# An attention and gated-MLP kernel: hand-set instruction order against a list scheduler with a time model

## The chip, the cores and the metric

The kernel runs on one core of a Trainium2 chip. The metric is the device time of one execution in microseconds (us), taken over several executions. The core has a matmul engine (PE, with weight loads listed as PEld), a vector engine (DVE), an activation engine (ACT), GpSimd (POOL) and a queue engine (SP) that issues the transfers. Each of them has its own instruction stream, whose order the program sets, and waits on semaphores for the others. The matmuls of this kernel write to PSUM, of which it uses eight banks. PE is called cold here where its granted clock was 0.50, half of full speed, and warm at 1.00.

A run is called slow when it is over 1.5% above the fastest of the same kernel in its set. The kernel before read between 619.6 and 631.7 us over all chips used here. Its profiled run, 629.58 us, carries the mark slow for that reason, in the set where 619.6 was the fastest; a fast run of a variant with the same early part shows the same early stretches (it is shown at its place below).

## The reference

```python
x  = A_x                                   # 1 x 2048 x 448, bf16
xn = layernorm(x)                          # no scale, no shift
q, k, v = split(xn @ wqkv)                 # 16 heads of 28
s  = softmax(q k^T / sqrt(28)) v, heads joined, @ wo
g  = silu(gelu(xn @ w1 + b1) @ w2 + b2)    # 448 -> 1792 -> 448
out = x + s * g
```

The 16 heads of 2048 x 2048 scores are 67 million exponentials. They run on ACT, 128 x 1536 at a time, in 342 instructions (the last is 128 x 512).

## The kernel before

Heads are packed four to a group, four groups, each head padded to 32 columns. A step `u` is three score matmuls of 512 columns, one exponential over the three PSUM banks they fill (a ring of six banks, so two steps), and three PV matmuls into the accumulator bank `acc`. Everything else (transposes of the normalised input, the projections K, Q and V, the MLP's first layer F1 and second layer F2, the softmax denominators, the output projection) is side work. It goes through the one bank that is left, `misc`, in generators that the main loop draws from by a fixed budget in ns per step:

```python
PV_LAG = 2
PV_START = 6
BUDGET0 = 900
BUDGET = 460
...
    def misc_item(self):
        return self.misc[:, :], self.b_misc
...
    def it_k(self, g, c):                   # K of head group g, chunk c of 512 rows
        bank, tok = K.misc_item()
        for k in range(2):
            K.proj_mm(1, g, c, bank, tok, (2 * k, 2 * k + 1))
            if k == 0:
                yield 440
        K.k_ev(DVE, g, c, bank, tok)
        yield 440
...
        for u in range(NU):                 # the main loop
            ...                             # scores of step u, exponential of step u, PV of step u - 2
            early = bool(fill) and u < 26
            bal = min(bal, 0) + (BUDGET0 if early else BUDGET)
            if gelu_it is not None and u == gelu_it + 2:
                bal += 22000
            while bal > 0:
                r = step_fill(u)
                if r is None:
                    break
                bal -= r
            if gelu_it is None and K.n_f1 == C * FT:
                gelu_it = u
                K.gelu()
```

Layernorm runs by chunks of four 128-row tiles: four statistics, one logarithm and one exponential on ACT for the four, four applications. GpSimd sets constants and pads from the start. At the end, the last head block's denominators go through GpSimd, and one dependence tracker per chunk covers the output buffer.

The softmax here doesn't subtract the row's maximum and nothing guards it: scores larger than these inputs give would overflow.

Of the kernel before, what the change touches and what calls it, by code (L numbers as in the profile page):

```python
# [14 lines left out]
D = 448  # L15
H = 16
DH = 28
F = 1792
G = 4
# [14 lines left out]
PV_LAG = 2  # L34
PV_START = 6
BUDGET0 = 900
BUDGET = 460


class _Buf:  # L40
    __slots__ = ("w", "r")

    def __init__(self):
        self.w = None
        self.r = []


class _Kernel:
    def __init__(self, nc, A_x, A_wqkv, A_wo, B_w1, B_b1, B_w2, B_b2, out):
        self.nc = nc  # L50
        self.A_x, self.A_wqkv, self.A_wo = A_x, A_wqkv, A_wo
        self.B_w1, self.B_b1, self.B_w2, self.B_b2 = B_w1, B_b1, B_w2, B_b2
        self.out = out
        self.es = ExitStack()
        self.prog = {PE: [], ACT: [], DVE: [], POOL: [], SP: []}
        self.evsem = {}
        self.evcnt = {}
        self.waited = {E: {} for E in self.prog}

# [16 lines left out]
    def own(self, E, h):  # L76
        return h is not None and h[0] is self.evsem[E]

    def deps(self, E, reads, writes):
        for b in reads:  # L80
            if not (E == PE and self.own(E, b.w)):
                self.wait(E, b.w)
        for b in writes:
            if not (E == PE and self.own(E, b.w)):
                self.wait(E, b.w)
            for r in b.r:
                if not (E == PE and self.own(E, r)):
                    self.wait(E, r)

    def mark(self, h, reads, writes):  # L90
        for b in writes:
            b.w = h
            b.r = []
        for b in reads:
            b.r.append(h)

    def emit(self, E, fn, reads=(), writes=()):
        self.deps(E, reads, writes)
        sem = self.evsem[E]
        self.evcnt[E] += 1  # L100
        self.prog[E].append(lambda eng, f=fn, s=sem: f(eng).then_inc(s, 1))
        h = (sem, self.evcnt[E])
        self.mark(h, reads, writes)
        return h

    def dma(self, E, fn, dsem, reads=(), writes=()):
# [4 lines left out]
        self.mark(h, reads, writes)  # L111
        return h

# [17 lines left out]
    def alloc(self):  # L131
# [18 lines left out]
        self.qsq = sb("qsq", [128, 512], bf)  # L150
# [4 lines left out]
        self.iota_f = sb("iota_f", [128, 128], f32)  # L155
# [22 lines left out]
        self.osb = self.h[:, :, 1792:3584].rearrange("p c (t d) -> p c t d", d=D)  # L178
        self.wsq = self.P[:, 20:24, :]
# [9 lines left out]
        self.b_xn = [B() for _ in range(3)]  # L189
        self.b_xnT = [[B(), B()] for _ in range(C)]  # L190
        self.b_stg, self.b_wv, self.b_w1, self.b_w2, self.b_wo = B(), B(), B(), B(), B()
# [10 lines left out]
        self.b_osb = [B() for _ in range(C)]  # L202
        self.b_E = [B(), B()]
        self.b_qsq, self.b_rc, self.b_rhl, self.b_colK, self.b_csq = B(), B(), B(), B(), B()
        self.b_wsq = [B() for _ in range(G)]
        self.b_st, self.b_mv, self.b_ln, self.b_rs = ([B() for _ in range(C)] for _ in range(4))
        self.b_fsb, self.b_sig = [B(), B()], [B(), B()]
        self.b_dum = B()
        self.s_x = [self.sem("s_x%d" % q) for q in range(4)]
        self.s_out = [self.sem("s_out%d" % q) for q in range(4)]  # L210
        self.s_w = {n: self.sem("s_" + n) for n in ("wqk", "wv", "w1", "w2", "wo", "b")}

    def schedule(self):
        self.constants()
        self.loads()
        self.startup()
        self.main()
        self.finish()

    def constants(self):  # L220
# [3 lines left out]
        def f(eng):  # L224
            eng.memset(K.epsc[:, :], LN_EPS)
            eng.memset(K.dum[:, :], 1.0)
            eng.memset(K.stg[64:128, 3, :, :, :], 0.0)
# [7 lines left out]
            eng.memset(K.ones[:, :], 1.0)  # L235
            return eng.memset(K.xn[:, :, :, D:512], 0.0)
        e(DVE, f, writes=[K.b_pads])

        def f(eng):
            return eng.memset(K.w1[64:128, 3, :], 0.0)  # L240
        e(DVE, f, writes=[K.b_w1])
# [5 lines left out]
        e(POOL, f, writes=[io])  # L247
# [3 lines left out]
        e(POOL, f, reads=[io], writes=[K.b_id])  # L251
        ec, tc = _Buf(), _Buf()
        e(POOL, lambda eng: eng.tensor_copy(K.ecol[:, 0:1], K.iota_p[:, :]), reads=[io], writes=[ec])
        for thr in (32.0, 64.0, 96.0):
            e(POOL, lambda eng, thr=thr: eng.tensor_scalar(K.tcol[:, :], K.iota_p[:, :], thr, 32.0,
                                                           op0=ALU.is_ge, op1=ALU.mult), reads=[io], writes=[tc])
            e(POOL, lambda eng: eng.tensor_tensor(K.ecol[:, 0:1], K.ecol[:, 0:1], K.tcol[:, :], ALU.subtract),
              reads=[ec, tc], writes=[ec])

        def f(eng):  # L260
# [3 lines left out]
        e(POOL, f, reads=[ec, io], writes=[K.b_cols])  # L264
        e(POOL, lambda eng: eng.tensor_scalar(K.tcol[:, :], K.ecol[:, 3:4], 28.0, None, op0=ALU.add),
          reads=[K.b_cols], writes=[tc])
# [4 lines left out]
        e(POOL, f, reads=[K.b_cols], writes=[hm])  # L271
# [4 lines left out]
        e(POOL, f, reads=[tc, hm, io], writes=[K.b_bsel])  # L276
# [3 lines left out]
        e(POOL, f, reads=[K.b_id], writes=[K.b_bsel])  # L280

        def f(eng):
            eng.memset(K.vaug[:, :, :, DH:DH + 1], 2.0)
            return eng.memset(K.vaug[:, :, :, DH + 1:32], 0.0)
        e(POOL, f, writes=[K.b_vpad])
        e(POOL, lambda eng: eng.memset(K.wo[:, :, :], 0.0), writes=[K.b_wo])
        self.prog[ACT].append(lambda eng: eng.preload_act_table_set("natural_log_exp_and_others"))

    def loads(self):
        K = self  # L290

        def ld(dst, src, sem, w):
            return K.dma(SP, lambda eng: eng.dma_start(dst, src), sem, writes=w)
        xr = K.A_x[0].rearrange("(c p t) d -> c p t d", p=128, t=4)
        wq = K.A_wqkv
        ld(K.x_sb[:, 0, :, :], xr[0], K.s_x[0], [K.b_x[0]])
        sf = K.stg.rearrange("p k w h d -> p k (w h d)")
        ld(sf[:, 0:3, :], wq[0:384, 0:2 * D].rearrange("(kt p) n -> p kt n", p=128), K.s_w["wqk"], [])
        ld(sf[0:64, 3, :], wq[384:448, 0:2 * D], K.s_w["wqk"], [K.b_stg])
        ld(K.x_sb[:, 1, :, :], xr[1], K.s_x[1], [K.b_x[1]])  # L300
        ld(K.wv[:, 0:3, 0:D], wq[0:384, 2 * D:3 * D].rearrange("(kt p) n -> p kt n", p=128), K.s_w["wv"], [])
        ld(K.wv[0:64, 3, 0:D], wq[384:448, 2 * D:3 * D], K.s_w["wv"], [K.b_wv])
        for c in (2, 3):
            ld(K.x_sb[:, c, :, :], xr[c], K.s_x[c], [K.b_x[c]])
        with K.nc.allow_non_contiguous_dma(reason="tiny bias load"):
            pass
# [4 lines left out]
        K.dma(SP, f, K.s_w["b"], writes=[K.b_b1])  # L311
        ld(K.b2b[:, :], K.B_b2.partition_broadcast(128), K.s_w["b"], [K.b_b2])
        K.b_b1.w = K.b_b2.w
        ld(K.w1[:, 0:3, :], K.B_w1[0:384, :].rearrange("(kt p) f -> p kt f", p=128), K.s_w["w1"], [])
        ld(K.w1[0:64, 3, :], K.B_w1[384:448, :], K.s_w["w1"], [K.b_w1])
        ld(K.w2[:, :, :], K.B_w2.rearrange("(ft p) d -> p ft d", p=128), K.s_w["w2"], [K.b_w2])
        K.wait(SP, K.b_wo.w)
        K.b_wo.w = None
        for hh in range(H):
            g, j = hh // 4, hh % 4  # L320
            ld(K.wo[32 * j:32 * j + DH, g, :], K.A_wo[hh * DH:(hh + 1) * DH, :], K.s_w["wo"],
               [K.b_wo] if hh == H - 1 else [])

    def ln_stats(self, c):
        K = self
        for t in range(4):
            i = 4 * c + t
            K.emit(DVE, lambda eng, i=i, t=t: eng.bn_stats(K.st6[:, i, :], K.x_sb[:, c, t, :]),
                   reads=[K.b_x[c]], writes=[K.b_st[c]])

        def f(eng):
            ins = None
            for i in range(4 * c, 4 * c + 4):
                ins = eng.bn_aggr(K.mv[:, i, :], K.st6[:, i, :])
            return ins
        K.emit(DVE, f, reads=[K.b_st[c]], writes=[K.b_mv[c]])

    def ln_rstd(self, c):
        K = self
        sl = slice(4 * c, 4 * c + 4)  # L340
        K.emit(ACT, lambda eng: eng.activation(K.lnv[:, sl], K.mv[:, sl, 1], ACTF.Ln, bias=K.epsc[:, 0:1]),
               reads=[K.b_mv[c], K.b_pads], writes=[K.b_ln[c]])
        K.emit(ACT, lambda eng: eng.activation(K.rstd[:, sl], K.lnv[:, sl], ACTF.Exp, scale=-0.5),
               reads=[K.b_ln[c]], writes=[K.b_rs[c]])

    def ln_apply(self, c):
        K = self
        for t in range(4):
            i = 4 * c + t
            K.emit(DVE, lambda eng, i=i, t=t: eng.tensor_scalar(  # L350
                K.xn[:, c % 3, t, 0:D], K.x_sb[:, c, t, :], K.mv[:, i, 0:1], K.rstd[:, i:i + 1],
                op0=ALU.subtract, op1=ALU.mult),
                reads=[K.b_x[c], K.b_mv[c], K.b_rs[c], K.b_pads], writes=[K.b_xn[c % 3]])

    def tr_mm(self, c, pr, bank, tok):
# [3 lines left out]
        def f(eng):  # L359
            ins = None  # L360
            for k in range(2):
                kt = 2 * pr + k
                for t in range(4):
# [3 lines left out]
        K.emit(PE, f, reads=[K.b_xn[c % 3], K.b_id], writes=[tok])  # L367

    def tr_ev(self, E, c, pr, bank, tok):
# [3 lines left out]
        if E == ACT:  # L373
            fn = lambda eng: eng.activation(dst, psb, ACTF.Copy)
        else:
            fn = lambda eng: eng.tensor_copy(dst, psb)
        K.emit(E, fn, reads=[tok], writes=[K.b_xnT[c][pr]])

    def proj_mm(self, which, g, c, bank, tok, kts=range(KT)):
        K = self  # L380
        kts = list(kts)
        w = (K.wq, K.wk)[which]

        def f(eng):
            ins = None
            for kt in kts:
# [14 lines left out]
    def v_mm(self, c, part, bank, tok):  # L401
# [12 lines left out]
        if part == 0:  # L414
            for q in range(2):
# [5 lines left out]
                if q == 0:  # L421
                    yield 500
# [553 lines left out]
```

## Time and profile before

| what | before |
|---|---|
| time, median of its runs | 629.93 us |
| span of the profiled run | 627.6 us |
| first exponential starts | 21.87 us |
| from there to gelu's table load (204 exponentials) | 347.0 us |
| gelu with its two table loads | 27.0 us |
| from there to the end of the last exponential (138) | 212.6 us |
| from there to the end | 19.1 us |
| ACT's waits for score matmuls before exponentials | 86.8 us |

The five stretches add up to the span. When ACT is full, exponentials stand 1.344 us apart, so 204 of them need 274.2 us and 138 need 185.5. What a stretch takes beyond that, 72.8 and 27.1 us here (with 6.8 us of tanh in the second), is what an order could save. The page, the cuts by stretch and the timelines that carry this are shown in the prediction.

### The profile page before, as it was taken

The page shows a single profiled execution, that of the slowest core. Times are in us where ns is not written, and L with a number is a line of the kernel's source. Part 1 is how long each engine was busy: PE and PEld are TensorE (multiplying, and loading weights), DVE is VectorE, ACT ScalarE, POOL GpSimd, SP SyncE. Part 2 cuts the span into 40 slices and gives each one's busy share as a digit, 9 for nine tenths or more (in the row PEclk, how much of TensorE's full clock was granted, in tenths as well). Part 3 has the DMA queues.
Part 4 walks back from the last instruction along what each step waited for, and adds up shares of the span by engine and source line. Part 5 has one row for each costly group of instructions (what it writes and reads, how often), then busy time and mean ns, then how long its engine had stood idle before and what let it go on. Part 6 is the DMA issues. An engine that isn't in the chain of part 4 may idle for free.

```text
span 627.6 us, 7506 instructions
## 1 busy us (share of the span) xinstructions
PE 494.6 (79%) x3074; PEld 142.9 (23%) x3106; DVE 177.8 (28%) x306; ACT 505.9 (81%) x367; POOL 55.6 (9%) x76
## 2 busy tenths in 40 slices
PE   1666778888887888898889848769899689898982
PEld 1232112322222222222222213312222112121220
DVE  7653223223323333323232311131111201121203
ACT  2443334987988999999999999468999999999970
POOL 8000100111110101010010100000010101010101
PEclk9775566997989999999999988978989655757766
DMA  8500000000000000000000000000000000000000
GB/s 257 174 2 1 0 0 1 2 0 1 1 0 2 2 1 1 1 1 0 2 1 1 0 1 0 2 0 2 1 0 1 1 0 2 30 0 30 1 29 29
DMA packets 7201, 9.07 MB, mean 14 GB/s; under 512 B 2304, under 2 KB 5824, under 8 KB 7168
## 3 DMA queue, kind: packets, MB, share of 16 engines
q1 hardware_dynamic: 7168, 8.61, 4.4%
q8 instruction: 24, 0.39, 0.2%
q14 instruction: 9, 0.07, 0.0%
HBM read 6.77 MB, written 1.84 MB: 14 GB/s over the span
## 4 chain that ended last, share of the span: by engine, by line
PE 48%; ACT 20%; DVE 19%; issue 12%; POOL 1%; DMA 0%; POOLq 0%; ACTq 0%; DVEq 0%
ACT P L836 18%; PE acc L784 9%; PE ring L821 9%; PE misc L594 8%; PE misc L629 6%; PE misc L387 6%; DVE h L604 5%; PE misc L410 2%; DVE h L350 2%; DVE qT L578 2%; DVE kT L398 2%; DVE qT L566 2%; PE misc L686 1%; PE misc L706 1%; DVE w L636 1%
## 5 line engine op out<-in xcount | busy, mean ns | idle before, releaser
L836 ACT ACTIVATE P<-ring 128x1536 bf16<-128x1536 f32 x342 | 466.6, 1511 | 87.4 <-PE ring L821 86.8
L821 PE MATMUL ring<-qT,kT 32*128 32x512 bf16 x1024 | 152.7, 440 | 24.7 <-ACT P L836 19.7
L784 PE MATMUL acc<-P,vaug 128*32 128x512 bf16 x1024 | 154.8, 446 | 1.3 <-DVE E_sb L658 1.3
L594 PE MATMUL misc<-xnT,w 128*128 128x512 bf16 x207 | 65.1, 393 | 18.9 <-DVE h L604 8.2
L629 PE MATMUL misc<-w,h 128*128 128x448 bf16 x224 | 56.6, 379 | 20.7 <-DVE w L636 12.0
L821 PEld LDWEIGHTS ring<-qT,kT 32*128 32x128 bf16 x1024 | 34.0, 93 | 163.0 <-ACT P L836 96.7
L604 DVE TENSOR_SCALAR h<-misc,b1c 128x512 bf16<-128x512 f32 x56 | 42.0, 750 | 102.1 <-PE misc L594 102.1
L784 PEld LDWEIGHTS acc<-P,vaug 128*32 128x32 bf16 x1024 | 34.3, 95 | 96.2 <-issue 91.5
L672 POOL CAST rhi<-rc 128x512 bf16<-128x512 f32 x16 | 9.8, 610 | 375.6 <-DVE rc L670 294.6
L636 DVE TENSOR_TENSOR w<-misc,b2b 128x448 bf16<-128x448 f32 x16 | 10.0, 624 | 82.2 <-PE misc L629 82.2
L567 POOL TENSOR_TENSOR qsq<-qT 128x512 bf16<-128x512 bf16 x15 | 15.6, 1039 | 182.0 <-DVE qT L566 182.0
L658 DVE CAST E_sb<-acc 128x512 bf16<-128x512 f32 x16 | 11.0, 690 | 68.7 <-PE acc L784 68.6
L629 PEld LDWEIGHTS misc<-w,h 128*128 128x128 bf16 x224 | 18.0, 100 | 48.3 <-issue 24.0
L410 PE MATMUL misc<-wv,xnT 128*128 128x128 bf16 (+1 forms) x128 | 21.2, 309 | 7.4 <-DVE kT L398 3.3
L387 PE MATMUL misc<-xnT,wk 128*128 128x512 bf16 x52 | 19.9, 465 | 8.0 <-DVE kT L398 2.1
L387 PE MATMUL misc<-xnT,wq 128*128 128x512 bf16 x57 | 21.2, 455 | 5.9 <-DVE kT L398 2.0
L613 ACT ACTIVATE h<-h 128x7168 bf16<-128x7168 bf16 x4 | 24.4, 6164 | 0.0
L594 PEld LDWEIGHTS misc<-xnT,w 128*128 128x128 bf16 x224 | 13.1, 98 | 45.8 <-DVE h L604 17.4
L566 DVE CAST qT<-misc 128x512 bf16<-128x512 f32 x15 | 10.4, 691 | 34.1 <-PE misc L387 34.1
L398 DVE TENSOR_SCALAR kT<-misc,ecol 128x512 bf16<-128x512 f32 x15 | 11.2, 749 | 28.9 <-PE misc L387 25.7
L691 DVE TENSOR_TENSOR qT<-misc,E_sb 128x512 bf16<-128x512 f32 x16 | 11.1, 692 | 29.4 <-PE misc L686 29.4
L439 DVE CAST vaug<-misc 128x336 bf16<-128x336 f32 (+1 forms) x20 | 10.6, 531 | 27.8 <-PE misc L410 27.8
(92 smaller groups left out, 233.0 us busy)
## 6 DMA issues: line engine op xcount, KB each, us to landing
x_sb<-in_A_x_dram SPq DMA_DIRECT2D x4, 448.0 KB, 6.3
w<-in_B_w_dram SPq DMA_DIRECT2D x1, 1568.0 KB, 12.1
w<-in_B_w_dram SPq DMA_DIRECT2D x1, 1344.0 KB, 7.4
out_dram<-h SPq DMA_DIRECT2D x3, 448.0 KB, 2.5
h<-in_A_wqkv_dram SPq DMA_DIRECT2D x1, 672.0 KB, 4.8
out_dram<-h SPq DMA_DIRECT2D x2, 224.0 KB, 1.9
wo<-in_A_wo_dram SPq DMA_DIRECT2D x16, 24.5 KB
wv<-in_A_wqkv_dram SPq DMA_DIRECT2D x1, 336.0 KB, 5.9
```

Source lines behind the costliest of these rows:

```text
L387: ins = eng.matmul(bank, w[:, kt, g * 128:(g + 1) * 128], K.xnT[:, kt, c * 512:(c + 1) * 512], start=(kt == 0), stop=(kt == KT - 1))
L398: fn = lambda eng: eng.tensor_scalar(dst, bank, K.ecol[:, 2:3], None, op0=ALU.add)
L410: ins = eng.matmul(bank[:, off:off + nh * 32], K.xnT[:, kt, t * 128:(t + 1) * 128], ap, start=(kt == 0), stop=(kt == KT - 1), skip_group_c ...
L566: K.emit(DVE, lambda eng: eng.tensor_copy(qb, bank), reads=[tok], writes=[K.b_qT[g][c]])
L594: ins = eng.matmul(bank, K.w1[:, kt, ft * 128:(ft + 1) * 128], K.xnT[:, kt, c * 512:(c + 1) * 512], start=(kt == 0), stop=(kt == KT - 1))
L604: K.emit(DVE, lambda eng: eng.tensor_scalar(dst, bank, K.b1c[:, ft:ft + 1], None, op0=ALU.add), reads=[tok, K.b_b1c], writes=[K.b_h[c]])
L613: K.emit(ACT, lambda eng, hv=hv: eng.activation(hv, hv, ACTF.Gelu_apprx_tanh), reads=[K.b_h[c]], writes=[K.b_h[c]])
L629: ins = eng.matmul(ps, hv[:, ft, t * 128:(t + 1) * 128], K.w2[:, ft, :], start=(ft == 0), stop=(ft == FT - 1))
L636: K.emit(DVE, lambda eng: eng.tensor_tensor(fb, ps, K.b2b[:, :], ALU.add), reads=[tok, K.b_b2], writes=[K.b_fsb[c % 2]])
L784: return eng.matmul(K.acc[32 * j:32 * j + 32, :], K.vaug[:, t, 4 * g + j, :], K.P[:, m % NP, :], tile_position=(0, 32 * j), start=(t == 0) ...
L821: return eng.matmul(K.ring[:, m % NRING, :], K.kT[32 * j:32 * j + 32, g, t * 128:(t + 1) * 128], K.qT[32 * j:32 * j + 32, g, c * 512:(c + ...
L836: return eng.activation(K.P[:, p0:p0 + n, :], K.ring[:, b0:b0 + n, :], ACTF.Exp, scale=SM_SCALE)
```

## The change

The intent: one list scheduler places the instructions of all engines. Every piece of work is a generator that yields tasks with an engine, the buffers read and written, a duration and a priority. The scheduler keeps a time for each engine and buffer and always places the task that can start earliest, lower priority number first among those on the same engine that start within 0.1 us. Scores have priority 1, PV 2, side work 5. With it come: layernorm by pairs of tiles, `acc` lent out as a second side bank until PV takes it, PV started by the scheduler, GpSimd's padding and weight squares held back until the normalised tile is there, the last denominator split on DVE, and output buffers tracked by halves.

```diff
+class _Task:
+    def __init__(self, E, fn, reads=(), writes=(), dur=0.1, lat=0.05, prio=5):
...
+    def start_of(self, t):
+        s = self.tE[t.E]
+        for b in t.reads:
+            if b.tw is None:
+                return None
+            s = max(s, b.tw + SEM)
+        for b in t.writes:
+            s = max(s, (b.tw or 0.0) + (0.0 if t.E == PE else SEM), b.tr + SEM)
+        return s
...
+            s0, p0 = min(cand, key=lambda c: (c[0], c[1][3].prio, c[1][0], c[1][1]))
+            E = p0[3].E
+            near = [c for c in cand if c[1][3].E == E and c[0] <= s0 + EPS]
+            s, p = min(near, key=lambda c: (c[1][3].prio, c[1][0], c[0], c[1][1]))
...
+        self.banks = [(self.misc[:, :], self.b_misc), (self.acc[:, :], self.b_acc)]
...
+    def p_k(self, g, c):
+        bank, tok = yield ("bank", lambda: K.ready(K.b_xnT[c] + [K.b_wqk[1][g]]))
+        for k in range(2):
+            yield K.t_proj(1, g, c, bank, tok, k)
+        yield K.t_kev(DVE, g, c, bank, tok)
+        K.banks.append((bank, tok))
...
+            yield ("until", lambda: K.exp_u >= u - 2)
+            yield _Task(PE, fall, rd, [K.b_ring[m % NRING] for m in ms], 0.31, 0.1, 1)
...
+        yield ("until", lambda: K.exp_u >= PV_START and any(t is K.b_acc for _, t in K.banks))
...
-        self.b_osb = [B() for _ in range(C)]
+        self.b_osb = [[B(), B()] for _ in range(C)]
...
+        En, d1, d2 = (DVE, 0.6, 0.65) if last else (POOL, 0.62, 1.05)
```

## The prediction

> **What bounds the kernel now.** I read the page first: shares, slices, groups.
>
> ```profile
> span 627.6 us, 7506 instructions
> ...
> PE   1666778888887888898889848769899689898982
> ...
> ACT  2443334987988999999999999468999999999970
> ...
> PEclk9775566997989999999999988978989655757766
> ...
> L836 ACT ACTIVATE P<-ring 128x1536 bf16<-128x1536 f32 x342 | 466.6, 1511 | 87.4 <-PE ring L821 86.8
> ```
>
> The softmax exponentials, 342 instructions on ACT, are the floor. ACT is nearly full in most slices and two thirds empty in slices 1 to 6. Its idle time before the exponentials, 86.8 us, is waiting for score matmuls (ring). Next I cut the exponentials by stretches: stretch, its length, ACT's busy time (count), clock.
>
> ```profile
> 22.00:60.00 38.00, 16.56 (x12) 0.69 0.07 19
> 60.00:110.00 50.00, 20.02 (x15) 0.59 0.00 0
> 110.00:160.00 50.00, 42.67 (x32) 0.90 0.00 1
> 160.00:240.00 80.00, 74.07 (x55) 0.98 0.00 1
> 240.00:369.00 129.00, 126.17 (x94) 1.00 0.00 1
> ...
> 396.00:430.00 34.00, 14.54 (x11) 0.80 0.00 1
> 430.00:606.00 176.00, 169.81 (x126) 0.76 0.02 9
> ```
>
> Of the waiting, 51.5 us lie in 22 to 110, about 13 in 110 to 240 (130 less 116.7, tiny operations left aside), and 16.4 in 396 to 430; hardly any from 240 to 369 or after 430. So the steady state is already bound by ACT: only start, gelu and end can give time. The timeline shows why the start is slow:
>
> ```profile
> 62.41 0.61 PE L821 MATMUL ring<-qT,kT 32*128 32x512 bf16 x3
> ...
> 63.49 1.03 PE L387 MATMUL misc<-xnT,wq 128*128 128x512 bf16 x2
> 64.56 0.69 DVE L566 CAST qT<-misc 128x512 bf16<-128x512 f32 x1 [3.18 <-PE misc L387]
> 65.31 1.03 PE L387 MATMUL misc<-xnT,wq 128*128 128x512 bf16 x2 [0.79 <-DVE qT L566]
> 66.28 0.61 PE L821 MATMUL ring<-qT,kT 32*128 32x512 bf16 x3
> ```
>
> Scores are 3.87 us apart though an exponential takes 1.45. Between them PE's in-order queue has two pairs of side matmuls (1.03 each), PV (0.61), and the wait for the one side bank's eviction (0.79). The before kernel sets side work by a fixed budget, 900 per step until step 26 and 460 after; at half clock, 900 is twice what it means.
>
> The span before adds up: first exponential at 21.87; 342 at 1.344 apart (score triples at 599.98, 601.33, 602.67: ACT full) 459.6; gelu with two table loads 27.0 (24.38 + 2 x 1.28); four tanh of 1.70, 6.8; layernorm activations between exponentials 1 (two pairs of 0.5); tail from the last exponential (608.48) 19.1. Sum 535.4. The missing 92.2 is the 86.8 of waits, plus about 0.1 for each of the 57 exponentials that did not follow another directly (1.45 against 1.344).
>
> **What the Trainium skill says.** "TensorE: Matmul & The Clock Gate", Part 1, has the array at half clock by default and full clock after a busy window of some 3.4 us. The trace agrees on two speeds: a score triple takes 0.61 at clock 0.50 and 0.39 at 1.00. It also shows that busy time at half clock need not lift it: 60 to 110 is 76% busy (37.97 of 50) at 0.59. "Perfetto Trace Analysis", Matmuls, advises rotating groups through PSUM banks; the 0.79 above is what one bank costs. "SBUF — State Buffer", Who interferes with whom, says that VectorE in its two-port modes and GpSimd exclude each other for whole instructions. The trace agrees: the four layernorm applications at 7.63 take 6.17 us beside GpSimd's memsets and multiply, the same four 1.68 at 22.76. "ScalarE: Activation LUTs", What ACT_TABLE_LOAD costs, says about 2.7 us; here it is 1.28, which decides.
>
> ```profile
> 7.63 6.17 DVE L350 TENSOR_SCALAR h<-x_sb,mv,rstd 128x448 bf16<-128x448 bf16 x4 [0.68 <-ACT rstd L343]
> ...
> 22.76 1.68 DVE L350 TENSOR_SCALAR h<-x_sb,mv,rstd 128x448 bf16<-128x448 bf16 x4
> ```
>
> **The change, part by part.** The arithmetic is nearly the same; order is what moves. I read the built order of both programs, no times from it.
>
> *Until the first exponential.* GpSimd's padding now waits for the normalised tile, so the four applications should cost 1.7, not 6.17: -4.5. Pairs let the second half's statistics run while ACT does the first half's rstd, but the second half waits on ACT behind a weight copy that needs a load landing at about 7: about -1. Against it, V matmuls (8 of 128 columns, 4 of 384, some 1.5 at half clock) now stand before the first scores: +1. First exponential at 17.4: -4.5. Four layernorm pairs now stand between exponentials: 2 in the sum below, where it was 1.
>
> *Steps 0 to 30.* Counted in the order, gaps between score groups with over 0.75 us of side matmul streaming (columns over 2.4 GHz) number 21 in steps 1 to 27 before and 7 after. Twelve of 64 matmuls for V's other heads stand in steps 20 to 40 where all 64 did; they spread to step 60. But three chunks' transposes, K and V must still come within 16 steps, and the largest gaps (2.13 at step 5, 1.49 at step 10, 1.28 at step 16) each cost one or two exponentials, double if cold. The second bank is used only until step 5: 5 groups of matmuls. PV starts after 5 score steps where it was 7, so "deferred" does not show as a later start. I book these two at 1 us or less. I leave 10 of the 51.5 idle us: -41, and 25 isolated exponentials become packed, -2.
>
> *Steps 30 to gelu.* One pair of side matmuls (about 0.45 warm) per step beside scores and PV (0.33 each), some 1.1 of 1.344, as in 240 to 369, where nothing idles. I leave 4 of 13: -9, with -2 for packing.
>
> *Gelu.* ACT's order has 212 exponentials ahead of it (204 before). Before, a bonus of 22000 put 150 F2 matmuls in front of the next scores, so ACT idled 10.9 us at once, 16.4 in all. Now F2 is spread, 54 to 56 matmuls per 20 steps over steps 220 to 280: 2.8 x 0.19 = 0.53 beside 0.66, which fits. K and Q of the last head group fill PE under gelu. I leave 2: -14, packing -1.
>
> *Tail.* Last PV 0.45; six output matmuls that stand ahead of the denominators, 2.25 at half clock (0.375 each); denominators and reciprocal 0.66; the split of the reciprocal on DVE 1.45 (estimate: as DVE's 0.69 for 512 columns, twice; it was 1.66 on GpSimd with handoffs); broadcast 0.6; multiply 0.75; first output matmul 0.6; four evictions of 1.14; store 2.0. Sum 13.3, against 19.1: -5.8. The 2.08 wait of DVE for the first store, visible below, goes, since the output buffer is now tracked by halves.
>
> ```profile
> 619.79 0.62 DVE L714 TENSOR_TENSOR h<-ring,h 128x448 bf16<-128x448 f32 x1
> 620.45 0.39 DVE L716 TENSOR_TENSOR h<-h,x_sb 128x448 bf16<-128x448 bf16 x1
> 622.93 0.62 DVE L714 TENSOR_TENSOR h<-ring,h 128x448 bf16<-128x448 f32 x1 [2.08 <-DMA out_dram<-h]
> ```
>
> Sum after: 17.4 + 459.6 + 27.0 + 6.8 + 2 + 13.3 = 526.1. Idle left: 10 + 4 + 2, and 2 for the stretch after 430, which I leave as it was: 18. The span is then 544.1. The differences added up (-4.5 - 43 - 11 - 15 - 5.8 = -79.3) give 548.3; they leave the other isolated exponentials as they are, so I take the sum. Runs exceed the span by 1.9 (629.43 to 629.58 against 627.6): **546 us**, a ratio of 0.867.
>
> **Rivals.** *The clock stays half.* The order was made with full-clock durations (0.31 for a triple). If PE stays cold with holes, a step costs 0.6 + 0.6 + 0.85 + handoffs, some 2.1, not 1.344, and 40 to 60 such steps cost 30 to 45: about 580. For: 60 to 110 is cold at 76% busy. Against: with a bank eviction covered by scores and PV, PE has no holes when cold, and the trace shows that full PE warms up (420 to 426 is 100% busy at 0.50, 432 on is 1.00). *The chunk chain in steps 0 to 16 is latency-bound* (layernorm, transpose, evict, project, evict through one bank): before, 22 to 60 had 12 exponentials in 38 us. If only PE's bursts shrink and this chain stays, 10 more us are lost: 555. *Packed solid*: if the order holds, idle falls to 6: 533. *A step order that fits a model but not the chip* makes small waits on every side group: 0.1 on 200 steps is 20: 565.
>
> **Range and chances.** All big terms are waits that the new order removes for plain reasons, with ACT's floor at 526 in span, 528 in time. Low: 532, nearly no idle. High: 562, the chain and some cold stretches. Being within 2% would need 70 of the 92 us to stay; a slower kernel would need new waits. Faster 0.97, same 0.02, slower 0.01.
>
> **What would show it.** First exponential near 17.4 and four applications near 1.7; 22 to 60 holding about 24 exponentials where it held 12; clock above 0.8 from 30 to gelu; no wait near 10.9 after gelu; tail near 13 with no DMA wait on DVE. I am wrong if the clock in 30 to 110 stays near 0.6, if the waits of exponentials for scores stay above 35 us, or if GpSimd now blocks DVE later on the path to the first scores.

## The result and the profile after

The changed kernel took 544.57 us (median of 4 runs, 544.18 to 547.09) against 629.93. The ratio is 0.8658, with a 95% interval of 0.8625 to 0.869. Ratios here are the mean time of one kernel's fast runs over that of the other's in the same rounds, so they are not quite the ratio of the medians quoted. The result was correct, and the profiled run was a fast one. The prediction had 546, and a range of 532 to 562.

The page of the changed kernel, the same lines as of before (busy tenths in 40 slices; PEclk is the clock granted to PE, in tenths of full speed; then the exponentials' group with its busy time, and the idle time ahead of it with what ended it):

```profile
span 542.9 us, 7525 instructions
...
PE   2778899999999999999999966899999998798973
...
ACT  3656999999999999999999999799999999999990
...
PEclk9887999999999999999999985899999999685867
...
L852 ACT ACTIVATE P<-ring 128x1536 bf16<-128x1536 f32 x342 | 462.3, 1851 | 12.5 <-PE ring L830 12.0
```

ACT is full from the fifth slice on (54 us), but for one slice behind gelu. The idle time ahead of the exponentials fell from 87.4 to 12.5 us. PE is busy 87% of the span, and its clock was 1.00 from 60 to 300 us. The exponentials by stretches (stretch, its length, ACT's busy time and count of exponentials, granted clock, two columns of transfers):

```profile
22.00:60.00 38.00, 24.23 (x18) 0.82 0.11 31
60.00:110.00 50.00, 50.00 (x39) 1.00 0.00 1
110.00:160.00 50.00, 50.00 (x39) 1.00 0.00 1
```

From 60 to 110 all 50 us are exponentials where it was 20.02, at clock 1.00 instead of 0.59. From 110 to 300 there is no gap at all. The stretch of 22 to 60 is the one that stays open: 24.23 busy of 38.

| what | before | after | difference |
|---|---|---|---|
| first exponential starts | 21.87 | 17.24 | -4.6 |
| to gelu's table load, beyond 1.344 per exponential | 72.8 | 15.0 | -57.8 |
| gelu and its table loads | 27.0 | 27.0 | 0 |
| from there to the last exponential's end, beyond 1.344 each | 27.1 | 9.9 | -17.2 |
| tail | 19.1 | 14.1 | -5.0 |

The differences sum to 84.6; the spans differ by 84.7. In the two rows of the exponentials, 211 and 131 stand after the change where 204 and 138 stood. ACT's timeline in the open stretch (start, duration, group, and the idle time just before):

```profile
17.24 4.13 ACT L852 ACTIVATE P<-ring 128x1536 bf16<-128x1536 f32 x3 [1.29 <-PE ring L830]
...
22.15 1.43 ACT L852 ACTIVATE P<-ring 128x1536 bf16<-128x1536 f32 x1
...
23.90 1.43 ACT L852 ACTIVATE P<-ring 128x1536 bf16<-128x1536 f32 x1
28.50 0.29 ACT L511 ACTIVATE lnv<-mv,epsc 128x2 f32<-128x2 f32 x1 [3.16 <-DVE mv L503]
...
30.66 0.30 ACT L511 ACTIVATE lnv<-mv,epsc 128x2 f32<-128x2 f32 x1 [1.64 <-DVE mv L503]
...
31.10 6.79 ACT L852 ACTIVATE P<-ring 128x1536 bf16<-128x1536 f32 x5
42.72 8.48 ACT L852 ACTIVATE P<-ring 128x1536 bf16<-128x1536 f32 x6 [4.82 <-PE ring L830]
53.80 67.27 ACT L852 ACTIVATE P<-ring 128x1536 bf16<-128x1536 f32 x50 [2.60 <-PE ring L830]
...
348.40 18.91 ACT L852 ACTIVATE P<-ring 128x1536 bf16<-128x1536 f32 x14 [2.76 <-PE ring L830]
```

The sixth exponential comes at 31.10, though the fifth ended at 25.33; there are waits of 4.82 before the eleventh and 2.60 before the seventeenth. From 53.80 to 315.87 exponentials follow each other without a gap. After gelu one wait of 2.76 us is left, and one of 0.50 at 479.

What PE did while the sixth exponential was waited for (the same columns, all engines):

```profile
24.33 1.86 PE L551 MATMUL misc<-xnT,wk 128*128 128x512 bf16 x4 [0.99 <-DVE xnT L542]
...
24.72 0.68 DVE L542 COPY xnT<-acc 128x1024 bf16<-128x1024 bf16 x1
...
27.95 0.13 PEld L551 LDWEIGHTS misc<-xnT,wk 128*128 128x128 bf16 x2 [0.84 <-DVE st L497]
...
29.73 0.75 DVE L562 TENSOR_SCALAR kT<-misc,ecol 128x512 bf16<-128x512 f32 x1
...
30.53 0.60 PE L830 MATMUL ring<-qT,kT 32*128 32x512 bf16 x6 [0.85 <-DVE kT L562]
```

PE works on a K projection at 24.33, then PV, then on a second K projection at 27.95, whose eviction ends at 30.48, and only then come six score matmuls. In the built order the first of these K projections waits for GpSimd, and GpSimd copies only the weights of the second to fourth head group. So the first one is K of a later group, not wanted before the 86th exponential (a group has four blocks of 64 score matmuls, three to a step). It got the side bank because it was ready when the bank came free; K of the second chunk, which the next scores read, was not ready yet (its second transposed half was evicted from 24.72 to 25.40) and had to wait for the bank, and then for PV's fifteen matmuls (26.13 to 28.03).

The time before the sixth exponential is not in the 12.0 us of waits for scores: ACT's stream has two layernorm pairs there, which wait 3.16 and 1.64 us for DVE. They end with the scores, not long after them. DVE's aggregate for the second pair (30.39) stands behind the eviction of that same K (29.73), and the first exponential started 0.44 us after its score matmuls (16.80 to 17.24); by that distance the sixth, with its scores at 30.53, would have come at 30.97 without layernorm, 0.13 us sooner.

The tail of the changed kernel:

```profile
529.30 0.61 PE L882 MATMUL acc<-P,vaug 128*32 128x512 bf16 x3
...
529.85 1.30 PE L943 MATMUL ring<-wo,qT 128*128 128x448 bf16 x3
...
531.09 0.41 PE L882 MATMUL acc<-P,vaug 128*32 128x512 bf16 x1
...
538.28 0.62 DVE L952 TENSOR_TENSOR h<-ring,h 128x448 bf16<-128x448 f32 x1
```

The last exponential ends at 528.77, but the last PV matmul stands behind two groups of three output matmuls and runs at 531.09. The third of the four output evictions (538.28) follows directly; before, it waited 2.08 us for the first store.

### The profile page after: what moved, and what is told of

It reads as the page before. It is cut to its first block, busy times and chain, and to the rows that moved or that the text cites. A ratio compares the mean times of both kernels' runs of the same rounds, so it can differ in the third digit from the quotient of the medians.

```text
span 542.9 us, 7525 instructions
## 1 busy us (share of the span) xinstructions
PE 469.9 (87%) x3106; PEld 138.4 (25%) x3106; DVE 174.2 (32%) x308; ACT 501.9 (92%) x375; POOL 53.9 (10%) x74
## 4 chain that ended last, share of the span: by engine, by line
ACT 55%; PE 22%; issue 15%; DVE 6%; DMA 1%; SPq 0%; ACTq 0%; DVEq 0%
ACT P L852 54%; PE ring L830 5%; PE acc L882 5%; PE misc L551 4%; PE misc L798 4%; PE misc L943 1%; PE misc L715 1%; DMA h<-in_A_wqkv_dram 1%; DVE kT L562 1%; DVE h L952 1%; DVE h L517 1%; PE ring L551 1%; DVE qT L691 1%; DVE qT L701 1%; PE misc L928 0%
## 5 line engine op out<-in xcount | busy, mean ns | idle before, releaser
L852 ACT ACTIVATE P<-ring 128x1536 bf16<-128x1536 f32 x342 | 462.3, 1851 | 12.5 <-PE ring L830 12.0
L830 PE MATMUL ring<-qT,kT 32*128 32x512 bf16 x1024 | 139.4, 403 | 32.6 <-ACT P L852 21.0
L882 PE MATMUL acc<-P,vaug 128*32 128x512 bf16 x1024 | 142.6, 411 | 0.9 <-ACT P L852 0.7
L755 PE MATMUL misc<-xnT,w 128*128 128x512 bf16 x224 | 66.6, 384 | 1.7
L798 PEld LDWEIGHTS misc<-w,h 128*128 128x128 bf16 x224 | 16.7, 100 | 28.7 <-issue 17.4
L551 PE MATMUL misc<-xnT,wq 128*128 128x512 bf16 x60 | 20.0, 433 | 3.8 <-DVE qT L701 2.5
L755 PEld LDWEIGHTS misc<-xnT,w 128*128 128x128 bf16 x224 | 13.3, 97 | 30.5 <-issue 13.2
L715 PE MATMUL misc<-wv,xnT 128*128 128x384 bf16 (+1 forms) x112 | 17.2, 294 | 0.3
L943 PE MATMUL misc<-wo,qT 128*128 128x448 bf16 x52 | 15.0, 387 | 2.4 <-DVE h L952 1.0
## 6 DMA issues: line engine op xcount, KB each, us to landing
w<-in_B_w_dram SPq DMA_DIRECT2D x1, 1568.0 KB, 14.1
```

What stands on the lines that cost most here:

```text
L551: ins = eng.matmul(bank, w[:, kt, g * 128:(g + 1) * 128], K.xnT[:, kt, c * 512:(c + 1) * 512], start=(kt == 0), stop=(kt == KT - 1))
L715: ins = eng.matmul(bank[:, off:off + nh * 32], K.xnT[:, kt, t * 128:(t + 1) * 128], ap, start=(kt == 0), stop=(kt == KT - 1), skip_group_c ...
L755: ins = eng.matmul(bank, K.w1[:, kt, ft * 128:(ft + 1) * 128], K.xnT[:, kt, c * 512:(c + 1) * 512], start=(kt == 0), stop=(kt == KT - 1))
L798: ins = eng.matmul(ps, hv[:, ft, t * 128:(t + 1) * 128], K.w2[:, ft, :], start=(ft == 0), stop=(ft == FT - 1))
L830: return eng.matmul(K.ring[:, m % NRING, :], K.kT[32 * j:32 * j + 32, g, t * 128:(t + 1) * 128], K.qT[32 * j:32 * j + 32, g, c * 512:(c + ...
L852: return eng.activation(K.P[:, p0:p0 + n, :], K.ring[:, b0:b0 + n, :], ACTF.Exp, scale=SM_SCALE)
```

## The experiments

Twelve runs, all correct. Each is timed against the kernel before in the same rounds. The rounds ran on three chips; across chips the ratios are the safer comparison. A scheduler that places everything anew also moves other work when one part is undone, so an undo is not the old state of that part alone. First come undos of single parts of the change.

**One side bank from the start.**

```diff
-        self.banks = [(self.misc[:, :], self.b_misc), (self.acc[:, :], self.b_acc)]
+        self.banks = [(self.misc[:, :], self.b_misc)]
...
-        yield ("until", lambda: K.exp_u >= PV_START and any(t is K.b_acc for _, t in K.banks))
-        i = [t is K.b_acc for _, t in K.banks].index(True)
-        K.banks.pop(i)
+        yield ("until", lambda: K.exp_u >= PV_START)
```

> The changed kernel with one PSUM bank for side work from the start; the accumulator bank is never lent. My theory, as predicted: the second bank carries only 5 groups of matmuls before step 5, so it is worth 1 us or less: 543 to 547 us, with the exponentials' waits for scores at 11 to 15 us instead of 12.0. Rival: the start was bound by the single bank, and the loan bought much of the early gain: 555 us or more, with waits of 22 us or more before 60.

Measured: 544.51 us (one of the four runs, 550.4, is slow and left out of the ratio), ratio 0.866 (0.8588 to 0.8731), waits of exponentials for scores 13.1 us. The second bank as the change uses it is worth nothing that these runs can tell. The rival falls.

**GpSimd's work early again.**

```diff
-            yield _Task(POOL, f, K.b_xn[0], [K.b_vpad], 1.6)
+            yield _Task(POOL, f, [], [K.b_vpad], 1.6)
...
-            yield ("until", lambda: K.ready(K.b_xnT[0]))
+            yield ("until", lambda: K.ready([K.b_stg]))
```

> The changed kernel with GpSimd's padding and weight squares at the start again, no longer held until the normalised tile is there. Theory: the two-port lock between VectorE and GpSimd returns, the first four layernorm applications take some 5 us instead of 1.5, the first exponential comes at 20 to 22 instead of 17.24, and all of it reaches the end: 548 to 550 us. Rival: the later chunks' chain is what sets the steps before 54, so a later first exponential is partly absorbed in the waits of 4.8 and 2.6 us that follow: 545 to 547 us.

Measured: 545.23 us, ratio 0.8686 (0.8627 to 0.8745). The scheduler put the weight square first, at 7.67, and the memsets after it. The square held up only the second pair of applications, which took 2.04 us instead of 0.70. The first exponential came at 18.78, and the seventeenth at 54.42 where it was 53.80. So the lock is there; in this order it takes 1.3 us from the first chunk and not 4.5, and the later chunks absorb most of it. The theory falls, the rival holds. The changed kernel does not escape the lock either: beside GpSimd's held-back copies and memset, three applications of its second chunk took 3.06 us (at 16.39), where here, with GpSimd done, they took 1.00 (at 17.83).

**Layernorm by whole chunk**, run twice.

```diff
-        for h in range(2):
-            for t in (2 * h, 2 * h + 1):
+        for h in range(1):
+            for t in range(4):
...
-        sl = slice(4 * c + 2 * h, 4 * c + 2 * h + 2)
+        sl = slice(4 * c, 4 * c + 4)
```

> The changed kernel with layernorm by whole chunk of four tiles instead of pairs. Theory: about 1 us later at the first exponential (18.2), and 1 us fewer small ACT operations, so 545 to 546.5 us in all. Rival: the pairs shorten every chunk's chain, so the waits of exponentials before 54 grow from 10 to 14 us or more: 548 us or more.

> The changed kernel itself, unedited, as the control for the next runs on the same chip: 543 to 547 us by the earlier runs, waits of exponentials for scores 11 to 14 us.

> The changed kernel with layernorm by whole chunk, once more, beside the control. If the pairs cost time (the first run read 542.3 us, with the wait before the sixth exponential shrunk), it is 2 us or more under the control. If that was run-to-run scatter of the loads and of PE's clock window, the two agree within 1 us.

Measured: 542.32 us, ratio 0.8641 (0.8576 to 0.8707), in the first run; 542.76, ratio 0.8655 (0.8612 to 0.8699), in the second, beside 545.45, ratio 0.8691 (0.8649 to 0.8732), for the unedited changed kernel on the same chip. The order of the two is the same both times, and the medians of the second pair differ by 2.7 us; the ranges just touch (541.76 to 544.56 against 544.23 to 545.97). So the pairs do not pay here. In the first run both theory and rival missed; in the second, the "2 us or more" held.

Where the time goes is not settled by the order alone. The changed kernel, its control and the run of the next experiment (whose edit touches only the end: the built PE streams agree in the first 2762 of 3151 instructions) have the same early order, with pairs. Their first exponentials came at 17.24, 16.19 and 17.03, against 17.39 and 18.00 with whole chunks. Their seventeenth came at 53.80, 54.95 and 51.30, against 50.10 and 50.61. PE from 42 to 48 us (stretch, its length, PE's busy time, clock), in the control and in the run of the next experiment:

```profile
42.00:48.00 6.00, 5.82 (x42) 0.50 0.01 3
...
42.00:48.00 6.00, 4.79 (x39) 1.00 0.00 0
```

The clock was 0.63 there in the changed kernel's profile and 1.00 in both with whole chunks. So at full clock the two orders are about 1 us apart at the seventeenth exponential, and the rest of the 4.3 us between control and whole chunks came with the clock. What set the clock, and whether pairs make the low one likelier, is open.

**The end undone.**

```diff
-        self.b_osb = [[B(), B()] for _ in range(C)]
+        self.b_osb = [[b, b] for b in (B() for _ in range(C))]
...
-        En, d1, d2 = (DVE, 0.6, 0.65) if last else (POOL, 0.62, 1.05)
+        En, d1, d2 = (POOL, 0.62, 1.05)
```

> The changed kernel with two parts of its end undone: one tracker per output tile group (so the second half waits for the first half's store) and the last split of the reciprocal on GpSimd again. Theory: tail from the last exponential 14.1 becomes 16.9 (2.1 from the store wait, 0.6 from the split with handoffs), 547 to 548 us in all. Rival: stores are not waited for when the order differs: 545 us.

Measured: 547.97 us, ratio 0.8725 (0.8669 to 0.8782), 3.4 us over the change. The tail was 17.9 us (528.13 to 546.0), 1 us longer than expected, and DVE waited 2.07 us for the first store again. The theory holds for the store. How much of the tail's other 1.7 us of growth is the split on GpSimd is not separated.

Then parts of the change done alone, on the kernel before.

**Less side work per step early.**

```diff
-BUDGET0 = 900
+BUDGET0 = 800
...
-            early = bool(fill) and u < 26
+            early = bool(fill) and u < 18
```

> The kernel before with less side work per step early on: 800 instead of 900, and only until step 18 instead of 26, then 460 as later. Theory A (too much side work is put between score groups, and half clock doubles it): of the 51.5 us of waits between 22 and 110, the part after 60 (32.5) shrinks to 12 or less, and the total falls to 600 to 610 us. Theory B (the waits come from one bank and PE's half clock, whatever the dose): the same groups still have to pass, the waits only move later, and the total stays at 622 us or more.

Measured: 596.9 us, ratio 0.9532 (0.9456 to 0.9607). The exponentials by stretches (columns as above):

```profile
22.00:60.00 38.00, 17.78 (x13) 0.91 0.10 25
60.00:110.00 50.00, 40.75 (x31) 0.90 0.00 1
```

Two constants give 31 us. The stretch of 60 to 110 doubled from 20.02 to 40.75 us of exponentials at clock 0.90, its waits fell from 32.5 to 10.6, and nothing of that came back later: the waits in all fell from 86.8 to 58.8. The stretch of 22 to 60 hardly moved. Theory A holds, and the total fell even below its range. PE was also busier than before (43.27 of 50 us from 60 to 110, against 37.97) and its clock higher, so the gain is that of the dose and of the clock that went with it; the run does not part the two. Smaller doses were not run on the chip. Some did not build (700 until step 18, 460 from the start), because a V or a K would then come after the step that reads it; others built (750 until step 18, 800 until step 10). So the best dose is not known.

**A smaller bonus after gelu.**

```diff
-                bal += 22000
+                bal += 2000
```

> The kernel before with the bonus after gelu cut from 22000 to 2000. Theory: F2 no longer stands in front of the next scores, the wait of 10.9 us after gelu falls under 3, and the waits after gelu fall from 16.4 to under 5: 614 to 618 us. Rival: F2 moved into later steps meets PE at half clock there and makes the exponentials wait, giving it back: 623 us or more.

Measured: 620.62 us, ratio 0.9911 (0.984 to 0.9982). The early part is untouched by this edit, so its stretches show in a fast run what the prediction read from before:

```profile
22.00:60.00 38.00, 15.96 (x11) 0.82 0.06 15
60.00:110.00 50.00, 18.86 (x13) 0.52 0.00 0
```

Busy 15.96 and 18.86 us here, 16.56 and 20.02 there. After gelu the waits from 396 to 432 fell from 16.4 to 1.1 us, as the theory said. But from 432 on they rose from 3.2 to 8.8, as the rival said. So each was half right: 15.3 gained, 5.6 given back. The profile of before that this is read against is slow (span 9.2 us longer); the fast runs differ by 5.5 us in the mean.

**Both constants.**

> The kernel before with both constants changed: 800 until step 18 instead of 900 until step 26, and a bonus of 2000 instead of 22000 after gelu. If the two gains stand in different stretches they add: 597 less 8 gives 587 to 592 us. If cutting the bonus only moves F2 to where PE is cold, 594 us or more. Either way the distance to the changed kernel, 45 us or so, is what the ordered schedule gives beyond a better dose.

Measured: 588.22 us, ratio 0.9362 (0.9319 to 0.9406). They add: ratios of 0.9532 and 0.9911 multiply to 0.945, and it was a little better still. Waits were 47.4 us. The changed kernel on the same chip took 545.45, so 42.8 us of the gain are beyond these constants as set here (a dose tuned further is a rival that was not run): 19.9 us of waits are left from 22 to 60 here against 7.4 that are named as waits for scores there, 18.1 from 60 to 240 against none, and the start and the tail are as before.

**A wrong time model.**

```diff
-        self.dur, self.lat, self.prio = dur, lat, prio
+        self.dur, self.lat, self.prio = dur * (0.7 if E == PE else 1.0), lat, prio
```

> The changed kernel with every PE duration in its time model multiplied by 0.7, so that the order is made for a PE that is 1.4 times too fast. Theory: steady steps have slack (PE needs about 1.1 of 1.344 us), so the denser order still nearly fits: 548 to 560 us, waits for scores 15 to 30 us. Rival 1: the order is brittle and each side group makes exponentials wait: 570 us or more. Rival 2: the durations do not matter, any order with scores first does it: 543 to 547 us.

Measured: 570.13 us, ratio 0.9104 (0.9026 to 0.9181). The waits, 24.1 us, are as the theory had them, but the time is Rival 1's. ACT's timeline in the steady part:

```profile
135.24 4.24 ACT L852 ACTIVATE P<-ring 128x1536 bf16<-128x1536 f32 x3 [0.28 <-PE ring L830]
139.76 4.24 ACT L852 ACTIVATE P<-ring 128x1536 bf16<-128x1536 f32 x3 [0.28 <-PE ring L830]
```

Three exponentials every 4.52 us, 1.507 each instead of 1.344: PE was given more side work per step than fits, and sets the pace. In such a group (134.80 to 139.33) it has eight side matmuls, and stands idle only for two waits of 0.20 for evictions from the side bank, at clock 1.00. From 60 to 240 this costs about 9 us (127 exponentials in 180 us; at 1.344 they need 170.7). The rest of the loss lies elsewhere, such as in a wait of 5.87 after gelu, and was not divided further. The gaps inside the groups add up too: the exponentials' busy time grew from 462.3 to 471.3. So the durations do matter; 25 us lie between a right and a wrong table of PE times, with the same rules. Factors of 1.3, 1.5 and 2.0 were tried as well and were refused before the chip, because two accumulations then came to stand open in one bank: the scheduler's dependences do not forbid that order, its usual durations merely avoid it.

Last, versions that mend what the trace showed.

**The mended kernel.**

```diff
-PV_START = 4
+PV_START = 6
...
-            K.spawn(K.p_v0(c), nxt())
+            if c > 1:
+                K.spawn(K.p_v0(c - 1), nxt())
...
-        bank, tok = yield ("bank", lambda: K.ready(K.b_xnT[c] + [K.b_wqk[1][g]]))
+        bank, tok = yield ("bank", lambda: K.ready(K.b_xnT[c] + [K.b_wqk[1][g]]) and (g == 0 or K.b_kT[0][C - 1].w is not None))
...
+            yield ("until", lambda: K.b_kT[0][C - 1].w is not None)
             yield K.relayout(POOL, 1, 1, 2, 0.6)
...
-        bank, tok = yield ("bank", lambda: K.sc_u == NU - 1 and len(K.banks) > 2 and K.g_done[c])
+        bank, tok = yield ("bank", (lambda: K.n_out == 4 * (C - 1) and K.g_done[c]) if t == 0 else
+                           (lambda: K.pv_u == NU - 1 and len(K.banks) > 2 and K.g_done[c]))
...
-        yield K.t_wo(ps, tok, c, t, (0, 1, 2), 8)
+        for g in range(3):
+            yield K.t_wo(ps, tok, c, t, (g,), 8)
```

The condition on the first group's last K is set for Q and V of later groups in the same way, and the memset of `wo` waits until step 24.

> The changed kernel, mended where its trace shows waits: side groups of the later heads (K, V, Q) get no bank until the first head group's K is through for all four chunks; V of a chunk comes after K of the next; PV takes its bank from step 6 instead of 4; GpSimd's later weight copies and memset are held back; the last output matmuls come singly, one tile early, the others after the last PV. Theory: a bank given too early to K of the second head group held up K of the second chunk: the waits of 5.8, 4.8 and 2.6 us before 54 fall to 7 in all, and the tail from 14.1 to 12.5: 537 to 541 us. Rival: those waits are the length of the chain itself on the chip: 543 to 546 us.

Measured: 536.89 us, ratio 0.8581 (0.8512 to 0.8651), some 8 us under the change and just below its range. The same place in its trace:

```profile
22.00 1.53 PE L555 MATMUL misc<-xnT,wk 128*128 128x512 bf16 x4
...
23.71 0.75 DVE L566 TENSOR_SCALAR kT<-misc,ecol 128x512 bf16<-128x512 f32 x1
...
24.51 0.60 PE L835 MATMUL ring<-qT,kT 32*128 32x512 bf16 x6
...
24.95 2.79 ACT L857 ACTIVATE P<-ring 128x1536 bf16<-128x1536 f32 x2 [0.63 <-PE ring L835]
```

K of the second chunk starts at 22.00, directly behind its transposes; it is evicted at 23.71, and the sixth exponential starts at 24.95 instead of 31.10. The tail was 12.6 us (520.71 to 533.3). Waits of 2.27 and 3.02 us before the eleventh and seventeenth exponential remain. The edits went in together, so how much PV's later start or GpSimd's delay did is not separated. PV from step 6 alone, without the rest, made a race on the side bank.

**The mended kernel with layernorm by whole chunk.**

> The mended kernel (side groups of later heads held back, later PV, single output matmuls at the end) with layernorm by whole chunk as well. If whole chunks help by themselves, 535 us or less and 9 us or more under the control; if not, 536 to 539 us.

Measured: 535.25 us, ratio 0.8533 (0.8492 to 0.8574), 10.2 us under the changed kernel on the same chip (545.45). It has the lowest median, but its interval overlaps that of the mended kernel with pairs (0.8512 to 0.8651), which was not on the same chip. The threshold of 535 was missed by 0.25 us, and the first exponential in its profile came at 19.44, late; the control's condition, 9 us or more, is met. So whether whole chunks help here too is not shown. The profiled run was its slowest, 537.71, and ACT's first weight copy waited in it until 8.41 for a load (6.71 in the mended kernel's).

## Why the prediction was right or wrong

The total was right (546 against 544.57), and its four gains were right in place and, within 4 us each, in size; inside two of them the causes were mis-sized. By the terms of the sum that gave 546: first exponential 17.4 predicted, 17.24 measured; beyond 1.344 per exponential before gelu 16 (10 and 4 of waits, 2 of layernorm), measured 15.0; after gelu 10.8 (waits of 2 and 2, tanh 6.8), measured 9.9; tail 13.3, measured 14.1. That the total came within 1.5 us is in part luck, since errors of both signs cancel, inside these terms too. Two counts were off without harm: 211 exponentials stand before gelu, not 212; and by the prediction's own terms a change within 2% (12.6 us), with 9.3 gained by start and tail, needs some 89 of the 92 us to stay, not 70.

**Floor and steady state.** Right. Exponentials at 1.344 us bound the span: no wait was left between 53.8 and 315.87, where the prediction still left 4 us. The clock was 1.00 from 60 to 300. Its step was a little too light: a pair of side matmuls, put at 0.45, took 0.54 in the trace of before (250.70 to 251.24), which makes 1.19 of 1.344 and still fits; F2's matmuls, put at 0.19, took 0.25 each in pairs (470.48 to 470.97). The first rival, a PE that stays at half clock, did not come.

**Steps 0 to 30.** The gain was right, its split was not. The dose of side work was the main cause: changing two constants moved 31 us, and 60 to 110 went from 15 exponentials to 31 in that run and to 39 after the change. But "22 to 60 holding about 24 exponentials where it held 12" failed: it held 18. (24 would leave 5.7 us idle in 38, fewer than the 10 that the sum left for 22 to 110.) The second rival, the chunks' chain, is in part what happened there; the trace names its worst link, the side bank given to a K of a later group, and the mended kernel, which forbids it along with its other edits, brought the sixth exponential 6.2 us earlier. What was too hopeful here and too cautious in the next stretch cancelled: 10 us left here and 4 in the next, 12.2 measured here (7.4 of waits for scores, 4.8 in front of layernorm's pairs) and none there.

**The start.** The place was right (17.4 predicted, 17.24 measured, 16.19 in the control's profile), and the four applications took 1.45 us where "near 1.7" was said. The cause was mis-sized. "-4.5" was booked on GpSimd's padding alone. Undone beside the pairs, it moved the first exponential by 1.5 us and the total by less than the scatter, because the pairs had already put two of the four applications ahead of GpSimd's multiply. With whole chunks and GpSimd held back, the four took 1.31 us, so the holding back can do it without the pairs as well; both undone together was not run. For the first exponential the pairs gave about the 1 us that was booked; in the total whole chunks read 2.7 us less, while in the profiles part of the difference came with PE's clock. The sign "GpSimd now blocks DVE later" did show, behind the first scores: 3.06 us for three applications at 16.39.

**Two banks, PV deferred.** "At 1 us or less" was right for the second bank as it is used (0.866 against 0.8658). The start of PV was not tested alone.

**Gelu.** Right: one wait of 2.76 where 2 was left, and 17.2 us gained after gelu where 15 was named. The experiment on the kernel before shows what the prediction did not say: the smaller bonus alone lost 5.6 of 15.3 later, while the changed order has only 0.5 us of waits in that later stretch.

**The tail.** 14.1 against 13.3. The store wait went as said (2.08 before, none after, 2.07 when undone). Two terms were off and nearly cancelled: "Last PV 0.45" was 2.7 (528.77 to the end of the last PV at 531.50), because output matmuls stood ahead of it; and "six output matmuls ahead of the denominators, 2.25" took 1.31 and hid for the most part behind the eviction of `acc`.

**A step order that fits a model but not the chip.** It did not come with the durations as given, but the experiment with PE at 0.7 shows the rival was real: 25 us.

## What to carry to other kernels

Read how much side work stands between two instructions of the bound engine, and in which clock it will run; a dose in ns that fits at full clock is too large when PE is cold (two side matmuls took 0.60 us at clock 1.00 and 1.03 at 0.50). A greedy scheduler gives a scarce bank to whatever is ready, so hold back work that is not yet due, and look in the trace for a late task that sat on the only buffer. A time model that sets the order must be close (30% off on one engine cost 25 us here), and the dependences must forbid every unsafe order, not only those that its durations happen to avoid.

## What the Trainium skill lacked or had wrong

- "TensorE: Matmul & The Clock Gate", Part 1, says that the clock rises after a busy window, but not how busy. In the kernel before, PE stood at clock 0.59 with 76% busy time (37.97 of 50 us, from 60 to 110). After the change it was busy 11.49 of 12 us from 500 to 512 at 0.70, then 5.89 of 8 at 1.00, then 6.34 of 8 (520 to 528) at 0.56. So busy shares near three quarters went with either clock, and no run isolates the share at which it rises or falls.
- "ScalarE: Activation LUTs", What ACT_TABLE_LOAD costs, has 1283 ns for the load, which the 1.28 us of each load here confirms, but about 2.66 us for every switch, with a drain in it. No drain shows here: after the change the last exponential before gelu ended at 315.85, the load ran from 315.87, and gelu started at 317.16.
- No page says that holding GpSimd's work back can move its lock with VectorE instead of removing it. Two layernorm applications took 2.04 us beside a GpSimd multiply (7.67 to 10.10) and 0.70 with that held back, but three later ones then took 3.06 us instead of 1.00. The total differed by 0.7 us, within the scatter.
